# Two hybrid layers on one core: in the first block the rows are normalized and turned ahead of the third raw chunk's folding, and a query tile's exponential and the third block's statistics are issued behind the keys' folding

## The chip, the core and the metric

The kernel runs on one core of a Trainium2 chip. The metric is device time in microseconds (us), smaller is better. Engines are called by the short names of the profile: PE is TensorE's matrix multiplication and PEld its weight load, DVE is VectorE, ACT is ScalarE, POOL is GpSimd, SP is SyncE, which issues the transfers. "L250" is line 250 of the kernel.

## The reference

Two layers, each of linear attention with a learned feature map and of a dense pair with Mish. Sequence S = 2048, width D = 640, 32 heads of 20, inner width F = 1536, everything in float32:

```python
def _A_ref(x, wqkv, w_phi, wo):
    q, k, v = split(x @ wqkv)                       # per head
    pq = einsum("bhsd,hdf->bhsf", q, w_phi); pk = einsum("bhsd,hdf->bhsf", k, w_phi)
    phi_q = concat([softmax(pq), softmax(-pq)])
    phi_k = concat([softmax(pk), softmax(-pk)])
    kv = einsum("bhsf,bhsd->bhfd", phi_k, v); z = phi_k.sum(over s)
    o = (phi_q @ kv) / (phi_q @ z + 1e-6)
    return o @ wo
def _B_ref(x, w1, b1, w2):
    h = x @ w1 + b1
    return (h * tanh(softplus(h))) @ w2
x = x + _A_ref(_layernorm(x), ...)
x = x + _B_ref(_layernorm(x), ...)                  # and both once more, same weights
```

## The kernel before

**Products.** Nearly every product is made of three in TensorE's fast float32 form: each operand is cut into a high part (a copy that rounds, made by ScalarE) and a low part (what is left, a subtraction on VectorE), and high·high, high·low and low·high are added up in PSUM. So each weight and each turned row exists twice, as a tile with h and one with l in its name (r2h, r2l: queries' weights; r1h, r1l: keys' and values' weights; xth, xtl: turned rows).

**Blocks.** The 2048 rows are worked on in 8 blocks of 256, each of two row tiles of 128. For attention a block is normalized (`norm_stats`, `norm_scale`, then `normed`), turned by TensorE's transposes (`Transposed.step`: four transposes, an ACT copy for the high part, a DVE subtraction for the low part; three steps make a block), and projected (`project_half`, L358, 15 matmuls of 320 columns) to keys, queries and values.

**Folding.** The map w_phi is multiplied into the query and key weights once, at the start of layer 0. The raw weights come transposed in six chunks of 120 (or 80) columns, `load_raw`; w_phi comes as block diagonals `bd`. `fold_part` (L240) multiplies a chunk by its diagonal into PSUM, one 128-row piece k and one chunk t at a time, and `fold_end` (L247) takes three chunks' result (columns 0 to 360, or 360 to 640) out of PSUM as a high and a low part. The queries' weights are folded in a hand-written part, the keys' by `fold_phi` (L253) before the first key tile's projection.

**Features.** A key or query tile passes through the stages of the generator `features` (L375), one stage for each call of `advance()`: ScalarE copies the projection from PSUM (L382 to L384), VectorE makes a maximum and a minimum over each head (L388), POOL (queries) or VectorE (keys) and VectorE again subtract (L389, L391), ScalarE takes the exponential (L394), VectorE sums and inverts (L397, L398), POOL multiplies (L399). A query tile is then transposed in blocks of 32 on VectorE (L444) and written to DRAM by four transfers (L448). Query tiles live in two buffers, r210 and r211, taken by turns (`query_tile`, L372), so each waits until the one before the last is written out. A key tile is multiplied with its values (L436) a few stages later.

**What sets the order.** The first block of layer 0 begins with a part inside `written()` (L467 to L521), in which the order of PE, SP, ACT, DVE and POOL is that of the source. Everything behind it is ordered by the compiler's scheduler, which simulates a timeline and sends each engine's instructions in the order of that; `tc.issue_after(x)` keeps what is made inside it behind the instruction x in that schedule. The helper `act` chains most of ScalarE's instructions in this way to the last one, `last_act[0]`. All engines take their instructions in order.

**PSUM.** Two kinds of tiles: "mm" with two banks, two in rotation, and "one" with one bank, four in rotation. The queries' folding takes both mm tiles for pieces 0 to 3 and a one tile for piece 4; the first projection takes the first mm tile again.

**The first block, in source order:** loads of rows, diagonals, chunks 0 to 2 of the queries' weights, then chunks 3 to 5, the values' weights (`fetch_v`), the keys' six chunks (`raw`), and the second block's rows (`early`); statistics; folding of chunks 0 to 2 for pieces 0 to 3; the first copy; the normalization of both row tiles (xn, ACT and DVE); the other copies with two steps of turning among them; piece 4; the third step; the first half of the first query projection; the chunks 3 to 5, with the splitting of the values' weights between them (`make_v`); the second half. Behind it the loop over blocks starts with the order q0, v0, v1, k0, q1, k1 (query, value or key, and row tile), with the keys' folding before k0. `fetch_normed` (L410) loads the rows of the next block and makes their statistics at the start of each block; the next block's rows are turned at places 3 to 5 of the order.

## Time and profile before

| | us |
|---|---|
| three runs | 1376.71, 1378.69, 1378.19 |
| median | 1378.19 |
| profiled execution, its own time | 1376.81 |
| its span on the core | 1375.0 |
| granted clock, mean | 0.999 |

The profile shows one execution on the one core; times inside it are counted from the start of its span, and its own time is 1.8 us above the span. The page's second part cuts the span in 40 slices of 34.4 us. PE has a 9 (90% or more) in every slice but the last. DMA moves 169.85 MB, 337 GB/s in the first slice, and 40 to 290 later. Of the five engines only PE is near its limit over the span; VectorE's slices lie between 5 and 9 tenths and the highest are the third, the fourth and five in the second half of the span.

The parts of the profile that the change touches lie in the first three slices. The rows that matter there are shown with the argument that uses them.

### The profile page before, as it was taken

What the parts mean: (1) busy time and instruction counts of PE and PEld (TensorE: products, weight loads), DVE (VectorE), ACT (ScalarE), POOL (GpSimd) and SP (SyncE); (2) the same over time, 40 slices, a digit from 0 to 9 for tenths busy, and PEclk for the clock granted to TensorE, in tenths of its full rate; (3) what the DMA queues carried; (4) which work ended last, traced back from release to release, by engine and by line L of the source; (5) the groups of instructions that cost most, each with busy time, mean ns of one, the idle gap of its engine ahead of it and who ended that gap; (6) DMA issues with size and microseconds to landing.
All of it is one profiled execution on the core that took longest, in us unless ns stands there. A gap on an engine that the chain in (4) does not pass through costs nothing.

```text
span 1375.0 us, 30860 instructions
## 1 busy us (share of the span) xinstructions
PE 1362.1 (99%) x12896; PEld 1349.8 (98%) x12896; DVE 1073.3 (78%) x1822; ACT 581.3 (42%) x970; POOL 441.0 (32%) x334
## 2 busy tenths in 40 slices
PE   9999999999999999999999999999999999999998
PEld 8999999999999999999999999999999999999998
DVE  5898877886688887788769899988678776677775
ACT  4344443222454545545444334332235444454443
POOL 1345553354322222122235434444242111111112
PEclk9999999999999999999999999999999999999999
DMA  9443424788614442244473433368975221333200
GB/s 337 148 95 62 75 40 96 204 242 292 224 55 97 116 105 77 59 107 99 141 245 77 85 59 64 67 132 270 285 253 151 77 59 41 94 97 96 69 29 20
DMA packets 350469, 169.85 MB, mean 124 GB/s; under 512 B 287209, under 2 KB 323801, under 8 KB 350329
## 3 DMA queue, kind: packets, MB, share of 16 engines
q1 hardware_dynamic: 350329, 167.88, 45.2%
q8 instruction: 101, 1.65, 0.5%
q14 instruction: 39, 0.32, 0.1%
HBM read 104.92 MB, written 62.91 MB: 122 GB/s over the span
## 4 chain that ended last, share of the span: by engine, by line
PE 96%; DMA 1%; DVE 1%; ACT 0%; issue 0%; DVEq 0%; SPq 0%
PE mm L364 29%; PE one L759 24%; PE mm L801 24%; PE one L364 12%; PE mm L637 3%; PE one L300 2%; PE one L436 2%; DMA v<-in_wv 1%; DMA r1l<-wp_d 0%; DVE r1l L251 0%; DVE bn L270 0%; ACT xn L129 0%; DVE r L397 0%; DVE xt L811 0%; ACT r L129 0%
## 5 line engine op out<-in xcount | busy, mean ns | idle before, releaser
L801 PE MATMUL mm<-r2h,ol 128*128 128x320 f32 x1280 | 305.0, 309 | 0.0
L785 POOL TENSOR_TENSOR ol<-big,ol 128x512 fp32r<-128x512 f32 (+1 forms) x98 | 129.9, 1326 | 483.7 <-ACT ol L784 409.3
L759 PE MATMUL one<-xtl,r1h 128*128 128x256 f32 x960 | 268.2, 279 | 0.0
L759 PE MATMUL one<-xth,r1l 128*128 128x256 f32 x960 | 268.0, 279 | 0.0
L759 PE MATMUL one<-xth,r1h 128*128 128x256 f32 x960 | 265.9, 279 | 0.0
L801 PEld LDWEIGHTS mm<-r2h,ol 128*128 128x128 f32 x1280 | 219.2, 188 | 0.3 <-ACT ol L784 0.3
L801 PE MATMUL mm<-r2l,ol 128*128 128x320 f32 x640 | 197.3, 309 | 0.0
L364 PE MATMUL mm<-r1h,xth 128*128 128x320 f32 x600 | 187.6, 313 | 1.6 <-DVE r1l L251 1.6
L364 PE MATMUL mm<-r1l,xth 128*128 128x320 f32 x600 | 185.8, 310 | 0.0
L364 PE MATMUL mm<-r1h,xtl 128*128 128x320 f32 x600 | 185.6, 310 | 0.0
L759 PEld LDWEIGHTS one<-xtl,r1h 128*128 128x128 f32 x960 | 180.4, 188 | 0.0
L759 PEld LDWEIGHTS one<-xth,r1l 128*128 128x128 f32 x960 | 180.4, 188 | 0.0
L759 PEld LDWEIGHTS one<-xth,r1h 128*128 128x128 f32 x960 | 179.6, 188 | 0.0
L774 DVE TENSOR_SCALAR big<-big 128x512 f32<-128x512 f32 (+1 forms) x98 | 57.1, 583 | 110.0 <-ACT big L772 109.8
L399 POOL TENSOR_TENSOR r<-r,r 128x1280 f32<-128x1280 f32 x32 | 77.7, 2429 | 156.4 <-DVE r L398 141.8
L801 PEld LDWEIGHTS mm<-r2l,ol 128*128 128x128 f32 x640 | 120.2, 188 | 0.0
L776 ACT ACTIVATE big<-big,two 128x512 f32<-128x512 f32 (+1 forms) x98 | 70.1, 716 | 116.1 <-DVE big L775 116.0
L772 ACT ACTIVATE big<-one,b1s 128x256 f32<-128x256 f32 x192 | 80.9, 468 | 89.0 <-PE one L759 88.5
L784 ACT ACTIVATE ol<-big 128x512 fp32r<-128x512 f32 (+1 forms) x98 | 60.9, 622 | 136.0 <-DVE big L783 135.9
L364 PEld LDWEIGHTS mm<-r1h,xth 128*128 128x128 f32 x600 | 112.8, 188 | 2.6 <-DVE r1l L251 1.8
L364 PEld LDWEIGHTS mm<-r1h,xtl 128*128 128x128 f32 x600 | 112.7, 188 | 0.2
L364 PEld LDWEIGHTS mm<-r1l,xth 128*128 128x128 f32 x600 | 112.8, 188 | 0.0
(133 smaller groups left out, 3119.9 us busy)
## 6 DMA issues: line engine op xcount, KB each, us to landing
e_d<-r SPq DMA_DIRECT2D x128, 160.0 KB, 4.0
big<-e_d SPq DMA_DIRECT2D x32, 640.0 KB, 7.6
x_d<-xt SPq DMA_DIRECT2D x23, 640.0 KB, 3.9
xt<-x_d SPq DMA_DIRECT2D x22, 640.0 KB, 5.5
n_d<-xn SPq DMA_DIRECT2D x176, 80.0 KB, 2.2
xt<-in_x SPq DMA_DIRECT2D x16, 640.0 KB, 4.4
xn<-x_d SPq DMA_DIRECT2D x28, 320.0 KB, 4.4
v<-n_d SPq DMA_DIRECT2D x30, 256.0 KB, 3.1
```

The lines of the kernel that those rows point to most:

```text
L300: nc.tensor.transpose(ps[:, c, t * P:(t + 1) * P], self.rows[t][:, (c0 + c) * P:(c0 + c + 1) * P], ident)
L364: nc.tensor.matmul(ps[:, :HC], a[:, sl], r, start=(k == 0 and n == 0), stop=(k == KD - 1 and n == 2))
L399: nc.gpsimd.tensor_tensor(eg, eg, r.unsqueeze(2).to_broadcast([P, 2 * H, DH]), op=ALU.mult)
L436: nc.tensor.matmul(kva[32 * j:32 * j + DH + 1, 40 * r:40 * r + 40], v[:, (DH + 1) * h:(DH + 1) * (h + 1)], e[:, 40 * h:40 * h + 40], start ...
L637: nc.tensor.matmul(po[64 * q:64 * q + 64, c, GW * j:GW * j + w], phs[g][:n, s0:s0 + 64], kvb[:n, g, :w], start=True, stop=True)
L759: nc.tensor.matmul(ph[:, j, :], l, r, start=(n == 0), stop=(n == 3 * KD - 1))
L772: exps[0] = nc.scalar.activation(part(ta, 0)[:, j - js.start], ph[:, j, :], AF.Exp, bias=b1s[:, 2 * pr + j:2 * pr + j + 1]).ins
L774: nc.vector.tensor_scalar_min(e, e, E_CAP)
L776: nc.scalar.activation(r, n, AF.Ln, bias=two)
L784: nc.scalar.activation(ah[:, js], n, AF.Copy)
L785: nc.gpsimd.tensor_tensor(al[:, js], n, ah[:, js].bitcast(F32), op=ALU.subtract)
L801: nc.tensor.matmul(pys[t][:, c, :HC], l[:, j, sl], r, start=(f == 0 and n == 0), stop=(f == KF - 1 and n == 2))
```

## The change

Three things are moved; no arithmetic is added or taken away.

1. In the hand-written part the normalization of the first block and the first two of its three steps of turning are issued ahead of the folding of the third chunk (t = 2); the copies of pieces 0 and 1 follow that folding, then the third step, then piece 4, then the copies of pieces 2, 3 and 4.
2. `fold_end` and `fold_phi` return the last ACT and DVE instruction of the folding. In block 0 the chain of ScalarE's instructions is continued from the folding's last copy, an `advance()` is called there, and the one after the third item of the order (v1) is left out. So the stage that was due after v1, the first query tile's exponential with what follows, comes behind the keys' folding.
3. In block 1 the loading of the third block's rows and their statistics are issued behind the folding's last low part.

```diff
     def fold_end(ws, ps, k, c):
...
-        nc.scalar.activation(hi, ps[:, :n1 - n0], AF.Copy)
-        nc.vector.tensor_tensor(lo, ps[:, :n1 - n0], hi.bitcast(F32), op=ALU.subtract)
+        a = nc.scalar.activation(hi, ps[:, :n1 - n0], AF.Copy)
+        v = nc.vector.tensor_tensor(lo, ps[:, :n1 - n0], hi.bitcast(F32), op=ALU.subtract)
+        return a.ins, v.ins
 
     def fold_phi(ws, bd, raw):
...
-            fold_end(ws, ps, k, c)
+            ends = fold_end(ws, ps, k, c)
+        return ends
...
-                for t in range(3):
-                    for k in range(KD - 1):
-                        fold_part(pcs[k], k, t, bd, raw_q)
-                fold_end(q_ws, pcs[0], 0, 0)
                 xn = [row_tile() for _ in range(BT)]
                 act(xn[0], xt[:, 0, :], AF.Identity, bias=stats[:, 0, 1, 0:1], scale=stats[:, 0, 0, 0:1])
                 nc.vector.tensor_scalar(xn[1], xt[:, 1, :], stats[:, 0, 0, 1:2], stats[:, 0, 1, 1:2],
                                         op0=ALU.mult, op1=ALU.add)
+                nxt = Transposed(xn)
+                for t in range(3):
+                    if t == 2:
+                        nxt.step()
+                        nxt.step()
+                    for k in range(KD - 1):
+                        fold_part(pcs[k], k, t, bd, raw_q)
+                fold_end(q_ws, pcs[0], 0, 0)
                 fold_end(q_ws, pcs[1], 1, 0)
-                fold_end(q_ws, pcs[2], 2, 0)
-                nxt = Transposed(xn)
-                nxt.step()
-                fold_end(q_ws, pcs[3], 3, 0)
                 nxt.step()
                 for t in range(3):
                     fold_part(pcs[4], 4, t, bd, raw_q)
-                nxt.step()
-                fold_end(q_ws, pcs[4], 4, 0)
+                for k in range(2, KD):
+                    fold_end(q_ws, pcs[k], k, 0)
...
+            begun = b == 0 and not layer
             for n, (kind, t) in enumerate(order):
...
                     if layer == 0:
-                        fold_phi(kv_ws, bd, raw)
+                        last_act[0], folded = fold_phi(kv_ws, bd, raw)
+                        advance()
...
                     if n == 0:
-                        xt = fetch_normed(b + 1)
+                        with tc.issue_after(folded) if b == 1 and not layer else nullcontext():
+                            xt = fetch_normed(b + 1)
...
                 next(g)
-                advance()
+                if not begun or n != 2:
+                    advance()
                 pending.append(g)
```

More of the change, by code (lines that the diff above doesn't have):

```diff
@@ L1 @@
-from contextlib import ExitStack, contextmanager
+from contextlib import ExitStack, contextmanager, nullcontext
 import concourse.bass as bass
```

## The prediction

> **What bounds the kernel now.** I read the page first, then TensorE's timeline, then the queues of the engines that release it.

> ```profile
> span 1375.0 us, 30860 instructions
> PE 1362.1 (99%) x12896; PEld 1349.8 (98%) x12896; DVE 1073.3 (78%) x1822; ACT 581.3 (42%) x970; POOL 441.0 (32%) x334
> ```

> TensorE is busy for 99% of the span. The change adds and removes no arithmetic, so only TensorE's holes can move the time: 1375.0 - 1362.1 = 12.9 us in all. Those in reach of the change lie in the first block.

> ```profile
> 11.59 1.27 PE L300 MATMUL one<-ident,xn 128*128 128x128 f32 x8 [0.92 <-ACT xn L126]
> 13.49 0.39 PE L364 MATMUL mm<-r2h,xth 128*128 128x320 f32 x1
> 15.71 0.35 PE L364 MATMUL mm<-r2l,xth 128*128 128x320 f32 x1
> 18.68 0.64 PE L244 MATMUL mm<-big,raw 120*128 120x120 f32 x4
> 34.81 0.39 PE L244 MATMUL one<-big,r 80*128 80x80 f32 x2
> 36.10 0.67 PE L244 MATMUL mm<-big,raw 120*128 120x120 f32 x4 [0.90 <-DVE r1l L251]
> 37.27 0.83 PE L244 MATMUL mm<-big,raw 120*128 120x120 f32 x6
> 37.94 0.82 PE L300 MATMUL one<-ident,xn 128*128 128x128 f32 x6
> 40.31 0.42 PE L364 MATMUL mm<-r1h,xth 128*128 128x320 f32 x1 [1.55 <-DVE r1l L251]
> ```

> Columns: start, duration, engine, line, operation, and in brackets the idle time and its releaser. Six folding records start within 37.94 - 37.27 = 0.67 us, 0.11 each; I measure holes start to start with that. At 34.81 two records are due to be followed at 35.03, but the next starts at 36.10: 1.07 lost. Six transposes from 37.94 are due to be followed at 38.60, and the next starts at 40.31: 1.71 lost. Together 2.78 us, both ended by VectorE writing low parts of the keys' folded weights. The first projection starts at 13.49.

> **Part one: the first block's rows ahead of the third chunk.** What it should remove is the 0.92 wait for xn, because ScalarE makes xn only behind a folding copy. The pieces:

> ```profile
> 8.43 0.23 DVE L282 SCALAR_TENSOR_TENSOR stats<-mv,stats 128x1 f32<-128x1 f32 x2 [1.10 <-POOL stats L280]
> 10.26 0.47 ACT L250 ACTIVATE r2h<-mm 128x360 fp32r<-128x360 f32 x1 [8.26 <-PE mm L244]
> 10.62 0.91 ACT L126 ACTIVATE xn<-xt,stats 128x640 f32<-128x640 f32 x1
> 10.76 0.53 DVE L251 TENSOR_TENSOR r2l<-mm,r2h 128x360 fp32r<-128x360 f32 x1 [2.10 <-ACT r2h L250]
> 12.45 0.60 ACT L126 ACTIVATE xth<-one 128x512 fp32r<-128x512 f32 x1 [0.20 <-PE one L300]
> 13.08 0.69 DVE L306 TENSOR_TENSOR xtl<-one,xth 128x512 fp32r<-128x512 f32 x1 [0.18 <-ACT xth L126]
> ```

> In the changed order ScalarE starts xn when the statistics end, at 8.66, and ends at 9.6. Four transposes are through at 10.15, the two xth copies end at 10.75 and 11.25, the first folding copy at 11.65. VectorE does both xtl first (11.45, 12.05), then the first low part (12.5). The two folded halves of one PSUM tile are handed over one after the other in the built order, so the second copy (0.47) and its low part (0.53) follow: 13.5. The projection's accumulator takes over that PSUM tile, so it starts at about 13.55, against 13.49. The earlier rows buy nothing; the low parts of later chunks cost another 0.1. So TensorE reaches the row of 15.71 at 15.8.

> There the built order has something new. The first folding of the keys' first chunk, which before is part of the four records at 18.68, stands in front of that product. TensorE takes instructions in order, so it waits until this chunk has landed.

> ```profile
> 11.28 3.60 SPq L236 DMA_DIRECT2D raw<-in_wqk_t  x5
> 17.93 0.33 SPq L404 DMA_DIRECT2D xt<-in_x  x1
> ```

> The chunk is the first of five loads issued from 11.28. The load at 17.93 takes the semaphore of the eighth load before it, which is that chunk, and waits for its landing: about 17.85. The loads ahead of it are issued as before, so the date stands. TensorE waits from 15.8 to 17.87, 2.05; with the 0.1 lost before, the front is 2.15 worse. From below this cost is nothing (if the load came 2 us sooner); from above 2.4 (if the last low parts of the queries' weights were waited for too). I take 2.15, which has a row for its end.

> **Part two: exponential and third statistics behind the keys' folding.** Ahead of the two holes the queues now hold, besides much else:

> ```profile
> 32.39 1.26 ACT L129 ACTIVATE r<-r 128x1280 f32<-128x1280 f32 x1
> 33.68 1.49 DVE L397 TENSOR_REDUCE r<-r 128x64 f32<-128x1280 f32 x1 [1.50 <-ACT r L129]
> ```

> Both go behind the folding, with the reciprocal, a transpose of the query tile and the statistics of the third and fourth block. What is left per folded chunk is 0.44 on VectorE (a 0.53 us low part, less overlap) and less on ScalarE, under TensorE's 0.67, and TensorE itself comes 2.15 later. I take both holes as gone: -2.78 (bounds 0 and -2.78). By 41 us the balance is -2.78 + 2.15 = -0.6 us.

> **Where the moved work goes.** VectorE has room behind the folding only for a short while:

> ```profile
> 40.00:50.00 10.00, 9.69 (x67) 9.69 (x68) 7.01 (x14) 1.60 (x3) 1.07 (x3) 1.00 0.87 222
> 50.00:60.00 10.00, 10.00 (x70) 10.00 (x69) 7.64 (x11) 3.96 (x6) 1.28 (x1) 1.00 0.24 80
> 60.00:70.00 10.00, 10.00 (x129) 9.75 (x128) 10.00 (x11) 6.57 (x9) 6.55 (x3) 1.00 0.20 66
> ```

> Columns: stretch and its length, then busy time (and instructions) of PE, PEld, DVE, ACT and POOL, the clock, DMA share, GB/s. VectorE is idle 3.0 and 2.4 us up to 60, and full from there. The moved work is some 7 us (statistics 2 x 1.6, sum 1.4, reciprocal 0.5, transpose 1.4, small ones), so the whole queue behind it comes late. Who waits for it: the second query tile (r, block 0, row tile 1). The built order also puts its GpSimd multiplication behind another tile's subtraction, and its transpose behind four bn_stats and two reductions more than before. It stays in its buffer until it is transposed and spilled, and the next query tile's copy needs that buffer.

> ```profile
> 43.59 0.45 DVE L251 TENSOR_TENSOR r1l<-mm,r1h 128x280 fp32r<-128x280 f32 x1 [0.71 <-ACT r1h L250]
> 68.59 1.50 DVE L444 STREAM_TRANSPOSE r<-r 128x1280 f32<-128x1280 f32 x1
> 70.12 3.39 SPq L448 DMA_DIRECT2D e_d<-r  x4
> 76.52 0.32 SPq L598 DMA_DIRECT2D ol<-e_d  x1
> 78.27 0.70 ACT L129 ACTIVATE r<-mm 128x640 f32<-128x640 f32 x1 [2.49 <-PE mm L364]
> 83.69 0.83 PE L436 MATMUL one<-big,v 128*21 128x40 f32 x64
> 84.45 0.41 PE L364 MATMUL mm<-r1h,xth 128*128 128x320 f32 x1
> ```

> Now: transposed by 70.09, four spills, and a load that waits for them goes at 76.52, 6.4 later. The copy at 78.27 waits for TensorE, with 1.75 to spare. In the changed order the date of the transpose is a sum over VectorE's queue, which has no gap in it:

> ```profile
> L388 DVE TENSOR_REDUCE m<-big 128x32 f32<-128x640 f32 x8 | 6.1, 801 | 3.6 <-ACT big L129 3.6
> L397 DVE TENSOR_REDUCE r<-big 128x64 f32<-128x1280 f32 x4 | 5.8, 1462 | 0.0
> L391 DVE TENSOR_TENSOR big<-m,big 128x640 f32<-128x640 f32 x4 | 4.6, 1144 | 0.0
> L398 DVE RECIPROCAL r<-r 128x64 f32<-128x64 f32 x6 | 3.2, 542 | 0.0
> L444 DVE STREAM_TRANSPOSE r<-r 128x1280 f32<-128x1280 f32 x2 | 3.0, 1478 | 0.0
> L270 DVE BATCH_NORM_STATS2 bn<-xt 128x6 f32<-128x320 f32 x4 | 1.7, 470 | 0.0
> ```

> It starts with the row of 43.59, now at 43.0 (-0.6). From there up to that transpose the built order has 12 reductions, 4 sums, 8 subtractions (0.81 unhindered), 4 reciprocals, 2 transposes, 12 bn_stats, 3 low parts and 9 short ones. Each occupies its mean less 0.08 of overlap: 8.7 + 5.5 + 5.9 + 1.85 + 2.8 + 4.7 + 1.5 + 1.1 = 32.0 us, so it ends at 75.0. To this come meetings with GpSimd:

> ```profile
> 64.23 2.37 POOL L399 TENSOR_TENSOR r<-r,r 128x1280 f32<-128x1280 f32 x1 [1.62 <-DVE r L398]
> 65.49 1.78 DVE L391 TENSOR_TENSOR big<-m,big 128x640 f32<-128x640 f32 x1
> ```

> The subtraction that began under GpSimd's multiplication ended 0.67 after it (67.27 against 66.60) and took 0.96 more than its 0.82. With GpSimd's three multiplications due before that transpose (query tile 0's, a key tile's, query tile 1's) I count three meetings. From below they cost 0; from above each the whole 2.37 + 0.67 - 0.82 = 2.2, together 6.6. I take 0.9 each as in the row: 2.7, so the transpose ends at 77.7. The spill lands 6.4 later, at 84.1, the copy ends at 84.8, and only then is the PSUM tile free that TensorE's product of 84.45 needs. By the built order TensorE is there at 84.45 - 0.7 (32 small products of 83.69 now stand behind) - 0.6 = 83.1, or a little sooner, 82.9. The new hole is 84.85 - 82.9 = 1.95; I take 2.1, since four spills in a queue have taken longer to issue elsewhere (3.75 for the first query tile). Behind 120 us the order on TensorE is the one of before.

> **Sum.** -2.78 + 2.15 + 2.1 = +1.5 us. The profiled execution took 1376.81 (its span 1375.0 and 1.8 around it), 1.4 under the median of the runs, 1378.19; so 1378.3 for its like, and 1379.7 as a median. A measurement of this kernel tells about 0.2% from no change, 2.76 us: my forecast is slower, but inside it.

> [...] All windows above show the granted clock at 1.00, across the hole of 1.71 too. [...]

> **Rivals.**
> 1. The spill stays hidden. If the meetings with GpSimd cost nothing, the transpose ends at 75.0, the copy at 82.1, before TensorE needs it. Then -0.6: 1377.6, not slower. For it: the schedule may interleave them cleanly; against: the 1.144 mean of L391 shows that meetings are common. 0.15.
> 2. The queue on VectorE runs later still: meetings nearer 2 us each, so the transpose at 80 or beyond, and the hole at 85 over 3.4. Then +2.8 to +5, 1382. It decides from 1.3 us more than I took. 0.26.
> 3. The keys' chunk is no wait (it lands by 15.8), and the spill is hidden: -2.8, 1375.4. Against it: the row of 17.93. 0.05.
> 4. The clock falls in or behind one of the holes. The row of warming transposes prices it: 30 in 5.1 us, 0.17 to 0.21 each, against 0.11 later, so some 2 us for a few us at half clock: +3.5, 1381.7. 0.04.

> ```profile
> 1.34 5.11 PE L89 MATMUL one<-ident 128*128 128x128 f32 x30 [1.34 <-POOL ident masks.py:199]
> ```

> **How the numbers follow.** My forecast has 0.50 (+0.3 to +2.7, that is 1378.5 to 1380.9). Of it and rival 1 nearly all lies within 0.2%; rivals 2 and 4 and the upper edge of the forecast are slower, 0.36; rival 3 is faster, 0.05; 0.59 remain. The range reaches down to rival 1 and up into rival 2: 1377.3 to 1382.4.

> **What would show it.** Right: a TensorE idle of about 2 us that a load of the keys' raw weights ends near 17.9; none at 35 to 40; one of about 2 us near 83 to 85 that ends with ScalarE's copy of a query tile, itself released by a spill. VectorE without a gap from 43 to 77. Wrong: the folding holes still there, no wait at 17.9, the spill's landing before 82, or holes beyond 120 us that the profile before doesn't have.

## The result and the profile after

| | before | changed |
|---|---|---|
| median of 13 runs, us | 1377.76 | 1381.67 |
| lowest and highest | 1376.62, 1379.43 | 1378.2, 1386.76 |
| profiled execution, its own time | 1376.81 | 1383.9 |
| its span | 1375.0 | 1382.1 |
| its mean granted clock | 0.999 | 0.995 |

The ratio of the runs is 1.003, with a 95% interval of 1.0021 to 1.0038: slower by 2.9 to 5.2 us, past the 0.2% that a measurement can tell. The runs of the changed kernel are spread three times as wide as those of before. Their mean granted clocks fall into two groups: eight executions at 0.998 to 1.000 with a median of 1380.35 us, and five at 0.994 to 0.996 with one of 1384.78. The profiled execution is of the second group.

TensorE's waits in the changed kernel, first; the columns are total, times, and the longest.

```profile
PE mm L244 <- DMA raw<-in_wqk_t: 3.1, 3, 1.8
PE mm L366 <- ACT r L129: 2.4, 1, 2.4
PE mm L366 <- DVE r2l L251: 1.3, 1, 1.3
```

The waits on r1l, the two holes at the keys' folding, are gone from the list. New are a wait of 1.8 for the keys' raw chunk, one of 2.4 for ScalarE's copy of a query tile, and one of 1.3 for a low part of the queries' weights ahead of the first projection, where before had the 0.92 for xn. TensorE's timeline places them (start, duration, engine, line, and in brackets the idle time and what ended it):

```profile
13.73 0.42 PE L366 MATMUL mm<-r2h,xth 128*128 128x320 f32 x1 [1.31 <-DVE r2l L251]
...
15.97 0.31 PE L366 MATMUL mm<-r2h,xth 128*128 128x320 f32 x1
18.07 0.75 PE L244 MATMUL mm<-big,raw 120*128 120x120 f32 x2 [1.79 <-DMA raw<-in_wqk_t]
18.49 0.61 PE L366 MATMUL mm<-r2l,xth 128*128 128x320 f32 x1
...
19.93 0.64 PE L244 MATMUL one<-big,r 80*128 80x80 f32 x2
20.36 1.06 PE L244 MATMUL one<-big,raw 120*128 120x120 f32 x4
21.21 0.64 PE L244 MATMUL one<-big,r 80*128 80x80 f32 x2
...
26.69 0.47 PE L366 MATMUL mm<-r2l,xth 128*128 128x320 f32 x1
26.95 0.47 PE L366 MATMUL mm<-r2h,xtl 128*128 128x320 f32 x1
...
42.85 0.87 PE L244 MATMUL mm<-big,raw 120*128 120x120 f32 x6
43.55 1.26 PE L302 MATMUL one<-ident,xn 128*128 128x128 f32 x10
44.57 0.39 PE L366 MATMUL mm<-r1h,xth 128*128 128x320 f32 x1
...
87.74 0.31 PE L366 MATMUL mm<-r1h,xtl 128*128 128x320 f32 x1
90.44 0.41 PE L366 MATMUL mm<-r1h,xth 128*128 128x320 f32 x1 [2.39 <-ACT r L129]
```

The folding at 42.85 runs into the transposes and the next projection without a wait. But look at the durations behind 18: the product at 18.49 takes 0.61 where those ahead of it take 0.31. TensorE's clock has been halved, to 0.50 from 17.89 on. The windows below are cut at the dates at which the trace's record of the granted clock changes (17.89 and 28.12), in steps of 3.41 us. The columns are the window and its length, the busy time of PE, PEld, DVE, ACT and POOL, the granted clock, and the transfers' share and GB/s.

```profile
14.47:17.89 3.42, 1.71 (x10) 1.18 (x9) 0.97 (x2) 0.83 (x2) 0.00 (x0) 1.00 1.04 397
17.89:21.30 3.41, 3.23 (x15) 3.26 (x15) 0.26 (x1) 0.40 (x1) 0.00 (x0) 0.50 1.07 318
21.30:24.71 3.41, 3.41 (x18) 3.41 (x17) 2.31 (x5) 2.32 (x5) 0.00 (x0) 0.50 1.03 341
24.71:28.12 3.41, 3.41 (x16) 3.41 (x16) 3.07 (x7) 2.67 (x6) 0.00 (x0) 0.50 1.04 408
28.12:31.54 3.42, 3.42 (x25) 3.42 (x24) 2.58 (x7) 0.11 (x1) 0.67 (x3) 1.00 1.03 405
```

A window of 3.4 us in which TensorE was busy for half of the time, 1.71 us, is followed by three at half clock. In them TensorE is called busy nearly throughout: busy at half speed, which the page's 99% doesn't show.

The span's 7.1 us can now be put together. The first product of the key projection behind the folding starts at 44.57, against 40.31 before: +4.26. The terms up to there: TensorE is through with what stood ahead of the row of 15.71 by 16.12, 0.41 later (0.24 of it because the first projection starts at 13.73 and not at 13.49); the folding product that now comes next starts at 18.07, 1.95 more. From 18.07 to 28.12 the clock is halved: six folding products take 1.28 us (19.93 to 21.21) where they took 0.67, and a product of 320 columns 0.26 (26.69 to 26.95) where it takes 0.15 at the full clock. So of these 10.05 us some 4.7 are lost, by an estimate from these steps. The two folding holes are gone, -2.78. Together +4.3. Behind 45 there is 7.1 - 4.26 = 2.8, of which the hole at 87.89 to 90.44 is 2.55.

Why that hole comes: VectorE, SyncE and ScalarE of the changed kernel.

```profile
47.82 0.45 DVE L251 TENSOR_TENSOR r1l<-mm,r1h 128x280 fp32r<-128x280 f32 x1 [3.03 <-ACT r1h L250]
...
55.93 1.75 DVE L391 TENSOR_TENSOR big<-big,m 128x640 f32<-128x640 f32 x1
...
70.41 1.60 DVE L391 TENSOR_TENSOR big<-big,m 128x640 f32<-128x640 f32 x1
...
75.19 1.91 DVE L393 TENSOR_TENSOR big<-m,big 128x640 f32<-128x640 f32 x1
...
81.19 1.50 DVE L446 STREAM_TRANSPOSE r<-r 128x1280 f32<-128x1280 f32 x1
```

```profile
82.71 3.97 SPq L450 DMA_DIRECT2D e_d<-r  x4
89.63 0.31 SPq L604 DMA_DIRECT2D ol<-e_d  x1
```

```profile
89.69 0.70 ACT L129 ACTIVATE r<-mm 128x640 f32<-128x640 f32 x1 [8.37 <-DMA e_d<-r]
```

VectorE goes without a gap from the last low part (47.82) to the end of the second query tile's transpose at 82.69. Three of its subtractions take 1.6 to 1.9 instead of 0.82. Only then is the tile spilled, the spill is through at 89.63, and the copy that needs its buffer ends at 90.39, 0.05 ahead of TensorE's next product.

### The profile page after: what moved, and what is told of

Same layout as the page of the kernel before. It is cut to its first block, busy times and chain, and to the rows that moved or that the text cites. A ratio compares the mean times of both kernels' runs of the same rounds, so it can differ in the third digit from the quotient of the medians.

```text
span 1382.1 us, 30857 instructions
## 1 busy us (share of the span) xinstructions
PE 1366.8 (99%) x12896; PEld 1354.3 (98%) x12896; DVE 1079.8 (78%) x1822; ACT 582.1 (42%) x970; POOL 440.7 (32%) x334
## 3 DMA queue, kind: packets, MB, share of 16 engines
q8 instruction: 101, 1.65, 0.5%
## 4 chain that ended last, share of the span: by engine, by line
PE 91%; DMA 1%; DVE 1%; ACT 0%; POOL 0%; issue 0%; SPq 0%; DVEq 0%; ACTq 0%
PE mm L366 26%; PE one L765 24%; PE mm L807 24%; PE one L366 11%; PE mm L643 3%; PE one L302 2%; PE one L438 2%; DMA raw<-in_w 0%; DMA v<-in_wv 0%; DMA e_d<-r 0%; POOL r1l L159 0%; SPq L450 0%; DVE big L393 0%; DVE bn L272 0%; DVE r L446 0%
```

## Experiments

Three theories stood against each other. The first: three separate things make up the result, namely one product ahead of its load at the front (with the clock's fall behind it), the folding holes gone, and a spill that comes late because the statistics and the exponential are both added to VectorE's queue. The second: the clock falls for another reason (the spill's hole, the 1.3 us hole at 13.7, or by chance). The third: one of the moved parts alone makes the query tile late. "Low clock" below counts executions with a mean granted clock of 0.997 or less.

| kernel | median us | before, run beside it | ratio, 95% interval | low clock |
|---|---|---|---|---|
| front alone | 1380.74 | 1377.87 | 1.0026 (1.0015 to 1.0037) | 3 of 12 |
| front undone | 1377.33 | 1377.87 | 0.9999 (0.9991 to 1.0008) | 0 of 11 |
| exponential alone | 1374.05 | 1377.87 | 0.9976 (0.9967 to 0.9985) | 0 of 10 |
| statistics alone | 1375.27 | 1377.87 | 0.9983 (0.9974 to 0.9992) | 0 of 11 |
| changed, folding held | 1379.08 | 1377.77 | 1.0006 (0.9998 to 1.0015) | 1 of 11 |
| front alone, folding held | 1378.98 | 1377.77 | 1.0012 (1.0003 to 1.002) | 3 of 11 |
| one product ahead, alone | 1385.42 | 1377.77 | 1.0047 (1.0031 to 1.0064) | 4 of 6 |
| both faults repaired | 1375.39 | 1377.58 | 0.9986 (0.9977 to 0.9995) | 0 of 11 |
| exponential, xn first | 1373.54 | 1377.58 | 0.9973 (0.9964 to 0.9982) | 0 of 10 |

### The front alone

The hand-written part as changed, everything else as before. Against the changed kernel:

```diff
-                        last_act[0], folded = fold_phi(kv_ws, bd, raw)
-                        advance()
+                        fold_phi(kv_ws, bd, raw)
...
-                        with tc.issue_after(folded) if b == 1 and not layer else nullcontext():
-                            xt = fetch_normed(b + 1)
+                        xt = fetch_normed(b + 1)
...
-                if not begun or n != 2:
-                    advance()
+                advance()
```

> The hand-written front as changed, the exponential and the statistics where they were. Theory (the front's wait for the keys' chunk pulls the clock down): the TensorE wait near 16 to 18 us stays, 1.7 to 1.9 us, and the granted clock is at 0.5 for some 10 us behind it in some executions; both holes at the keys' folding (1.07 and 1.71) come back, no hole near 90; executions with a mean clock of 0.998 or more are 2.2 to 2.6 us slower than before, those with 0.997 or less 6 to 8 us slower. Rival (the clock falls because of the spill's hole near 90, or by chance of the chip): every execution keeps a clock of 0.998 or more and the time is at most 2.6 us above before.

Three of 12 executions are at 0.996, with a median of 1384.72, the nine others at 1380.06: 2.2 us above before, and 4.7 more with the low clock. In the profiled execution the load came sooner and the wait was 0.7, less than expected, and the clock stayed up; the folding holes are back.

```profile
PE mm L364 <- DVE r1l L251: 1.8, 1, 1.8
...
PE mm L244 <- DMA raw<-in_wqk_t: 1.2, 2, 0.7
...
PE mm L244 <- DVE r1l L251: 0.8, 1, 0.8
```

So the low clock comes with the front alone, without the parts moved behind it. No profile of this kernel caught such a fall; that it is the fall behind the front's wait rests on its size, 4.7, near the 4.7 lost above. A folding hole, back here, was followed by half clock too (the front alone with the folding held, below), but for some 2.5.

### The front undone

The front of before, with the changed kernel's other parts: the same as the diff of the change without its part in the hand-written order.

> The front of before, with the exponential and the third block's statistics behind the keys' folding. Theory: no wait near 16 to 18, no folding holes (-2.8), the hole behind the query tile's spill stays (2.5 to 2.8, now near 83 us), the clock stays at 0.998 or more in all executions; time within 0.5 us of before. Rival (the clock falls because of the spill's hole): some executions show a clock of 0.997 or less and are 4 to 6 us slower.

The time is that of before, and no execution has a low clock. The profile shows where the gain of the folding holes goes.

```profile
PE mm L366 <- ACT r L129: 2.7, 1, 2.7
```

```profile
79.99:83.40 3.41, 1.11 (x7) 1.11 (x8) 3.41 (x5) 1.86 (x3) 2.72 (x2) 1.00 0.17 38
83.40:86.82 3.42, 3.42 (x74) 2.98 (x72) 3.38 (x6) 1.61 (x5) 3.42 (x3) 0.50 0.00 0
86.82:90.23 3.41, 3.41 (x25) 3.41 (x24) 2.15 (x3) 0.80 (x2) 3.41 (x2) 1.00 0.36 58
```

Of the hole of 2.7, 2.3 us lie in one window here, and the clock is halved for the window behind it, at most 3.4 / 2 = 1.7 us more by an estimate from the 0.50. That is not in the mean clock beyond its third digit (0.998 in this execution), so the expected bound of 0.998 holds although the reason behind it does not: the spill's hole was followed by half clock too, only for 3.42 us and not for the 10.2 at the front.

### Exponential alone, statistics alone

Both with the front of before. One keeps the new place of the exponential, the other that of the statistics:

```diff
 # exponential alone
-                        with tc.issue_after(folded) if b == 1 and not layer else nullcontext():
-                            xt = fetch_normed(b + 1)
+                        xt = fetch_normed(b + 1)
 # statistics alone
-                        last_act[0], folded = fold_phi(kv_ws, bd, raw)
-                        advance()
+                        folded = fold_phi(kv_ws, bd, raw)[1]
...
-                if not begun or n != 2:
-                    advance()
+                advance()
```

> The front of before, only the exponential behind the keys' folding; the third block's statistics where they were. Theory (VectorE's queue holds too much only when both are moved): both folding holes go and the spill lands in time, no hole over 0.5 us near 80 to 90; 2.3 to 2.9 us faster than before. Rival (the exponential is what makes the query tile late): the hole near 83 stays, 2 us or more, and the time is within 0.6 us of before. Second rival (the holes at the folding need both parts gone): one hole of 1.0 to 1.7 stays at 35 to 40.

> The front of before, only the third block's rows and statistics behind the keys' folding; the exponential where it was. Theory: the four bn_stats (1.65 us) are gone from ahead of the folding's low parts, and that is enough: both folding holes go, no hole over 0.5 us near 80 to 90; 2.2 to 2.8 us faster than before. Rival (the sum over the query tile, 1.49 us, which waits for the exponential, is what holds the low parts up): one or both folding holes stay, and the gain is 1.1 us or less.

Each of the two takes both folding holes away, and neither has a wait at 80 to 90. The statistics alone are 2.6 us faster than before (1377.87 - 1375.27), the exponential alone 3.8. The latter is more than expected, and why is not shown: its profile is shorter by 2.9 (1375.0 - 1372.1), of which 0.7 is a raw chunk of the queries' weights that landed sooner, so that TensorE waited 0.2 for it instead of 0.9. With the statistics alone there is no wait for it at all, so this difference belongs to the execution rather than to what was moved. The date of the query tile's transpose and of the load behind its spill tell why there is no hole; first the exponential alone, then the statistics alone:

```profile
69.33 1.45 DVE L446 STREAM_TRANSPOSE r<-r 128x1280 f32<-128x1280 f32 x1
```

```profile
78.36 0.32 SPq L603 DMA_DIRECT2D ol<-e_d  x1
```

```profile
65.65 1.50 DVE L446 STREAM_TRANSPOSE r<-r 128x1280 f32<-128x1280 f32 x1
```

```profile
73.85 0.32 SPq L602 DMA_DIRECT2D ol<-e_d  x1
```

With both moved and the same front the transpose stands at 72.74 and the load goes at 81.48; TensorE is due at 79.4 there. So the spill is late only when both are added to VectorE's queue, and one of them is enough for the folding.

### The changed kernel with the folding held

The keys' folding products are tied behind the last product of the first half projection:

```diff
-                fold_part(ps, k, t, bd, raw)
+                with tc.issue_after(half):
+                    fold_part(ps, k, t, bd, raw)
...
-                project_half(q0[0], nxt, 0, q_ws, 0, 0)
+                half = project_half(q0[0], nxt, 0, q_ws, 0, 0)
```

> The changed kernel with one thing more: the products that fold the keys' raw weights stay behind the last product of the first half projection. Theory (the front's loss is that one product standing ahead of its load, and the clock falls because of the wait that comes of it): no wait over 0.3 us between 15 and 18.5 us, no execution with a mean clock of 0.997 or less; the 1.3 us hole at 12.4 to 13.7 and the spill's hole (2.4 to 2.8, with at most one window at half clock behind it) stay; 0.3 to 1.6 us slower than before. Rival (the 1.3 us hole at 13.7 is enough to bring the clock down): some executions show 0.997 or less and are 4 us above the others.

The wait at 16 to 18 is gone, and 2.6 us with it (1381.67 to 1379.08). Against the expectation one execution has a low clock, 0.997; it is 1.7 above the others' median of 1379.02, the price of one window and not of three. The hole at 13.7 stands here too (the same 1.31), in front of no low clock like that of the changed kernel. Left is the spill's hole, and in the profile it lies in one window and halves the clock for the next.

```profile
PE mm L367 <- ACT r L129: 2.6, 1, 2.6
PE one L89 <- POOL ident masks.py:199: 1.3, 1, 1.3
PE mm L367 <- DVE r2l L251: 1.3, 1, 1.3
```

```profile
80.79:84.20 3.41, 0.78 (x6) 0.74 (x6) 3.41 (x5) 1.49 (x2) 2.75 (x1) 1.00 0.27 54
84.20:87.62 3.42, 3.42 (x55) 3.09 (x58) 3.39 (x6) 1.98 (x5) 3.27 (x2) 0.50 0.00 0
```

### The front alone, with the folding held

The same tie on the kernel that has the changed front alone.

> The changed front alone, with the same tie: the keys' folding products stay behind the first half projection; exponential and statistics where they were. Theory: the earlier rows give no time (the projection starts 0.1 to 0.3 us later than before), both folding holes come back with nearly their old size; no wait at 16 to 18, no clock of 0.997 or less; 0.3 to 1.6 us slower than before. Rival (the earlier rows do help once the wait is away): 0.5 to 1.0 us faster than before.

1.2 us slower than before, in the range, so the rows' new place costs and does not help. The clock was a miss: three of 11 executions are at 0.997, 2.5 us above the others. Its profile, at 0.998 not counted among them, shows what such a fall looks like, behind the larger folding hole:

```profile
39.05:42.46 3.41, 1.63 (x13) 1.40 (x12) 3.33 (x11) 0.42 (x1) 1.86 (x1) 1.00 1.02 393
42.46:45.87 3.41, 3.41 (x16) 3.41 (x15) 1.74 (x5) 0.23 (x1) 1.08 (x3) 0.50 0.64 184
45.87:49.29 3.42, 3.42 (x25) 3.42 (x24) 0.64 (x2) 1.11 (x3) 0.00 (x0) 1.00 0.91 142
```

The kernel of before has that hole as well, and 5 of its 77 runs beside these kernels stand at 0.997. So the folding holes are probably worth a little more than their own length; the one profile of before has no such fall.

### One product ahead of its load, alone

The kernel of before, with the keys' first folding product in the place that it has in the changed kernel:

```diff
-                project_half(q0[0], nxt, 0, q_ws, 0, 0)
+                project_half(q0[0], nxt, 0, q_ws, 0, 0, range(KD - 1))
+                ahead = mm_tile()
+                project_half(q0[0], nxt, 0, q_ws, 0, 0, (KD - 1,), lambda: fold_part(ahead[:, 0], 0, 0, bd, raw))
...
-                fold_part(ps, k, t, bd, raw)
+                if k or t:
+                    fold_part(ps, k, t, bd, raw)
```

> The kernel of before with one product moved: the first folding product of the keys' first chunk stands in front of the last two products of the first half projection, as in the changed kernel; everything else as before. Theory (this one product is the front's whole cost): a wait of 2.0 to 2.4 us that ends with the load near 17.9; executions with a clock of 0.998 or more are 1.6 to 2.6 us slower than before, and since the wait is a little longer than in the changed kernel, a third or more of the executions show 0.997 or less and are 4 to 5 us above the others. Rival (the clock falls only where the 1.3 us hole at 13.7 stands ahead of the wait): no execution of 0.997 or less. Second rival (the folding holes at 35 to 40 take up the delay): less than 0.8 us slower.

Only six runs, but they are plain: two at 1379.16 and 1381.08 with a clock of 0.999 and 1.000, and four at 0.994 to 0.996 with a median of 1385.66, 5.5 above, a little more than the 4 to 5 expected. One product's place in the order costs 2.4 us in the first group, which is two runs 1.9 apart, and 8 in the second. The profiled execution is the slower of the two, and has besides a wait of 1.7 for a ScalarE copy (ol), which is 0 to 1.3 in the other profiles here and whose cause is not shown; comparisons of about 1 us between two profiles have to be read with that in mind. Its clock stayed up:

```profile
17.43 0.45 PE L244 MATMUL mm<-big,raw 120*128 120x120 f32 x2 [2.09 <-DMA raw<-in_wqk_t]
```

```profile
13.27:16.69 3.42, 2.08 (x13) 1.62 (x11) 1.79 (x4) 0.75 (x3) 0.00 (x0) 1.00 1.03 394
16.69:20.10 3.41, 2.67 (x23) 2.70 (x24) 0.58 (x2) 0.97 (x3) 0.00 (x0) 1.00 1.06 365
```

This wait, 2.09, is longer than the 1.79 of the changed kernel's profile, and the clock stays: the windows, counted here from the date at which the clock was first granted in full, cut it in two, and both parts have TensorE busy for over half, 2.08 and 2.67 us. The 1.3 hole at 13.7, which this kernel doesn't have, is not needed for the fall: four of its six executions are at 0.994 to 0.996.

### Both faults repaired

The changed kernel with the folding held, and the statistics in their old place.

> The changed kernel with both faults taken out: the keys' folding products stay behind the first half projection, and the third block's statistics stay where they were (only the exponential goes behind the folding). Theory: no wait at 16 to 18, no folding hole over 0.6 us, no hole over 0.5 us near 80 to 90, no execution with a clock of 0.997 or less; 1.0 to 2.2 us faster than before, so some 1 us short of the exponential alone, which is the later start of the first projection. Rival (the changed front gains once its wait is gone): as fast as the exponential alone or faster, 3 us or more below before.

2.2 us faster than before and without a low clock. It stays behind the exponential with xn first, run beside it, by 1375.39 - 1373.54 = 1.85 us; the start of the first projection in the two profiles is 1.89 apart (the first row is of the repaired kernel, the second of the other):

```profile
13.58 0.42 PE L367 MATMUL mm<-r2h,xth 128*128 128x320 f32 x1 [1.31 <-DVE r2l L251]
```

```profile
11.69 0.41 PE L366 MATMUL mm<-r2h,xth 128*128 128x320 f32 x1 [0.28 <-ACT xth L126]
```

### The exponential, and xn ahead of the first copy

The exponential alone, and of the changed front only what its hole asks for: ScalarE and VectorE make xn ahead of the first folding copy, and the transposes stay behind the third chunk.

```diff
-                fold_end(q_ws, pcs[0], 0, 0)
                 xn = [row_tile() for _ in range(BT)]
                 act(xn[0], xt[:, 0, :], AF.Identity, bias=stats[:, 0, 1, 0:1], scale=stats[:, 0, 0, 0:1])
                 nc.vector.tensor_scalar(xn[1], xt[:, 1, :], stats[:, 0, 0, 1:2], stats[:, 0, 1, 1:2],
                                         op0=ALU.mult, op1=ALU.add)
+                fold_end(q_ws, pcs[0], 0, 0)
```

> The exponential alone behind the folding, with the front of before but for one step: the normalization of the first block stands ahead of the first folding copy on ScalarE and of its low part on VectorE. Theory (the front is limited by ScalarE's and VectorE's copies as a whole, not by the rows): the 0.9 us wait for xn near 11.5 goes, and waits of together 0.6 to 0.9 us come at 12.5 to 13.5 for the first folded piece and its low part; within 0.4 us of the exponential alone. Rival (the rows are the limit): the projection starts 0.8 to 1.0 us sooner and stays ahead, 3.2 us or more below before.

The 0.92 wait for xn is gone, and smaller waits follow in its place: the 0.28 in the row above and 0.19 behind it. They end with the two parts of the turned rows, xth and xtl, and not, as the theory had it, with the first folded piece.

```profile
12.45 0.41 PE L366 MATMUL mm<-r2h,xtl 128*128 128x320 f32 x1 [0.19 <-DVE xtl L308]
```

The gain over the exponential alone is in between the two expectations: 0.65 us in the profiles from 15 us on, 0.2 of which is the wait for the queries' raw chunk that this profile doesn't have, and 0.5 by the medians, whose intervals overlap. At 4.0 us below before it has the lowest median of all the kernels here.

## Why the prediction was right, and where it was wrong

**Right, with its size.** The load that TensorE runs into at the front (predicted: from 15.8 to 17.87; the folding product due at 16.12 started at 18.07). The front's loss: the one product alone is 2.4 above before where the clock stays (two runs), and 2.15 was forecast. Both folding holes are gone, -2.78. The queue on VectorE: 34.7 us were summed from the last low part to the end of the transpose (43.0 to 77.7), and it took 34.9 (47.82 to 82.69). Of the three meetings with GpSimd, for which 2.7 was taken, the three long subtractions took (1.75 + 1.60 + 1.91) - 3 x 0.82 = 2.8 more.

**Mis-sized.** The spill's hole: 2.1 forecast, 2.55 measured (2.7 with the front undone). The difference lies in the spill itself, 6.9 from the end of the transpose to the next load, where 6.4 was taken from before. The late start of the first projection was 0.24 and not 0.06, and the row of 15.71 was due 0.41 later and not 0.1.

**The step that failed.** The sum has no term for a fall of the clock. That holes of 2.05 and 2.1 leave it up was the author's estimate, and the runs speak against it: a wait of 1.79 in the changed kernel's profile and one of 2.70 with the front undone were followed by half clock, though one of 2.09 with the one product alone was not. The clock was a rival of its own (the fourth, 0.04, +3.5 us, 1381.7), and it decides a quarter or more of the executions with the wait at the front: 5 of 13, 3 of 12 with the front alone, and 4 of 6 with the one product alone. In the eight other executions of the changed kernel it is 2.6 us slower than before (1380.35), inside the forecast's own +0.3 to +2.7. The measured median of +3.9 mixes the two. The price was too low too: the fall was costed by the 30 warming transposes, some 2 us for a few us at half clock, and it holds for 10.2 us here and costs some 4.7. So "slower inside 0.2%" was not the outcome, and the chance of 0.04 and the price of this rival are what the sum had wrong. That the range of 1377.3 to 1382.4 held the median of 1381.67 is in part luck: its upper end was there for rival 2, which did not happen.

**Rival 2**, a later queue on VectorE with a hole over 3.4 (the 2.1 taken and 1.3 more), gives nearly the same time for another reason, and did not occur: the queue was as summed. Rivals 1 and 3 fell with the rows at 90.44 and 18.07.

**What the change was worth.** Its idea behind the folding was sound and doubled: one of its two halves is enough, and the second only fills VectorE's queue until the query tile's buffer comes too late. Its front as a whole gave nothing: the folding held, it costs 1.2 us (front alone, folding held). With the rows turned early, the start of the projection waits 1.31 for a low part of the folded weights. Only xn ahead of the first copy gained, some 0.5 us by the last experiment.

## What to carry to other kernels

Where a scheduler fills in around a hand-written part, read the built order of the engine that bounds the kernel for instructions that have slipped ahead of their loads: here one small product cost 2.4 us, and 8 with the clock. Move just enough out of the way of a wait, and then ask which buffer the moved work releases later. Price an idle time of TensorE by the half clock that can follow it as well (here, by estimates, up to 1.7 us for one window of it and some 4.7 for three), and compare runs together with their mean clocks: a clock halved in five of 13 executions showed up as a spread of 1378.2 to 1386.76.

## What the runs showed of the hardware

In the changed kernel's profile the record of the granted clock has changes at 4.23, 17.89, 28.12 and 1379.80, which are 4, 3 and 396 steps of 3.413 us apart; in that of before it has them at 4.70 and 1373.45, 401 such steps apart. In the changed kernel's profile a single wait of 1.8 us, 1.6 of it in one window, was followed by half clock. Of the windows measured behind the first grant of the full clock, the four that left TensorE 2.2 us or more idle were followed by half clock (2.3 us of idle with the front undone, 2.6 with the folding held, 2.2 and 3.0 where the products thin out at the program's end, in the changed kernel and in that of before). At 1.7 to 1.8 both outcomes occur: a fall behind 1.71 in the changed kernel and 1.78 in the front alone with the folding held; none behind this window of the front alone, 1.76:

```profile
38.43:41.84 3.41, 1.65 (x14) 1.21 (x12) 3.34 (x10) 1.15 (x3) 2.36 (x1) 1.00 1.02 392
```

Unexpected too: how long it takes to come back. With the front alone and the folding held, and with the front undone, the falls at 42 and 83 us ended after one window; in that at 83.40 products of 320 columns ran for 2.0 us. That at 17.89 lasted three. In the second of its windows, 21.30 to 24.71, TensorE was busy throughout (3.41 us), with folding products of 80 to 120 columns alone, and the clock stayed at half; it returned at the end of the third, in which the half projections had begun again at 26.27. So a window called busy was not enough here. That the folding products are small is no sufficient reason: at the start of the program the clock was granted in full, at 4.23 in the changed kernel's profile and 4.70 in that of before, behind a window with nothing but warming transposes of 128 columns (16 in the 3.36 us up to 4.70, 0.21 each, and the other 14 in the 1.75 behind). What tells the two kinds apart is open; no run tried it.
